# A two-branch state-space kernel: the middle stage of its long convolution in 64x32 and 32x64 pieces without an exchange of halves, transposes in 64x64 quarters, and a new order

## The chip, the cores and the metric

The kernel runs on one core of a Trainium2 chip. The metric is the time of one execution in microseconds of the device (us), of which lower is better. The core has a matrix engine (TensorE: PE for its matmuls, PEld for its weight loads), a vector engine (VectorE, DVE), an activation engine (ScalarE, ACT), a general engine (GpSimd, POOL) and a synchronization engine (SyncE, SP). SP and POOL issue the transfers. The engines run side by side, each through its own instructions in a fixed order, and wait for each other by semaphores.

## The reference, cut to what matters

Two independent branches of 2048 positions by 1024 channels in bfloat16, put side by side in the output:

```python
def _A_ref(q, k, v, shift_k, ssm_k, ssm_D):      # branch A
    # k_shift: k run through a filter of 4 taps along the positions
    kv = k_shift * v
    # convolution of kv with ssm_k along 2048 positions, by a Fourier transform of length 4096
    kv_f = rfft2(pad(kv)); kf_f = rfft2(pad(ssm_k)).transpose(...)
    y = irfft2(kv_f * kf_f)[:S] + kv * ssm_D
    return q * y

def _B_ref(x, Lambda, B, C, log_dt, Dskip):      # branch B
    Bu = einsum("bld,pd->blp", x, B_bar)          # B_bar complex
    h[t] = Lam_bar * h[t - 1] + Bu[t]             # 1024 complex states, 2048 steps
    y = 2.0 * einsum("blp,dp->bld", h, C).real + x * Dskip
```

## The kernel before, in words

**Branch B** works in 16 chunks `i` of 128 positions. A transfer that transposes brings a chunk of x (`x.i`). `U.i.jp.jl` (line 464) multiplies it by B, 16 matmuls of 128x128 by 128 columns, and two of them fill one PSUM bank; `ue` (line 473) copies the bank to SBUF. `r1`, `r2` (lines 487 and 498) turn the states, `sc` (line 504) scans along time, `r3`, `r4` turn them back. The output product by C is `y.i.dh.part` (line 520, whole 128x128 weights) in chunks 0, 1, 2, 14 and 15, and `yq.i.k` (line 538, in quarters of 64x64, four of which run at the same time) in chunks 3 to 13. `ye` (line 556) copies the result, `yst`, `ysp`, `ysh`, `ysg` store it.

The weights of B and C arrive row by row (`bl`, `cl`), are transposed on PE by `bT`, `cT` (both through `tr_`, line 415, eight 128x128 blocks into one bank), and are copied out of PSUM by `bc` (line 431, ACT), `bcv` (DVE) and `cc` (line 439, ACT). Eight of the sixteen blocks of C are transposed by a transfer instead (`cx`, line 437).

**Branch A** does its Fourier transform of 4096 as 128 times 32, in three stages through DRAM.
- First stage. `kvm`, `kva`, `kvb`, `kvc` (lines 588 to 603, DVE) filter k and multiply by v for sixteen groups of positions `n2`; `am` (line 608) transforms them, 4 matmuls a group, `ae` (line 614) copies, `ast` (line 617) stores to `Ys_kv`. The filter `ssm_k` is transposed on PE by `hT` (line 632, eight 128x128 blocks a bank), copied by `hc` (line 637, ACT), transformed by `hm` (line 657, quarters of 64x64), copied by `he` (line 665), stored to `Ys_h` by `hst` (line 668).
- Middle stage, the one that is changed: 16 steps `i` of two groups `g`. `lh`, `lk` load both transforms, `lw` (line 672) loads that step's weights. `s2` (line 688, called as `sh` and `sk`) does the transform of 32 for one group: 4 matmuls of 64x64 by 512 columns, which end in two banks, real and imaginary parts on neighbouring partitions. `she` (line 697) and `ske` (line 704) copy the banks. The complex product needs the filter's parts in both orders, so `sw`, `swp` (line 708; the first issued by POOL, the second by SP) write a second copy with neighbouring partitions exchanged, by a transfer from SBUF to SBUF, two a step. `pr` (line 714, DVE) multiplies both copies by the data's transform, 4096 elements a partition. `sa` (line 726) transforms back, 8 matmuls of 64x64 by 512 columns for a group, two rounds of four. `sae` (line 734) copies, `vst` (line 737) stores to `Vs`.
- Last stage. `vl` loads, `a3` (line 754) transforms, `a3e` (line 761) copies, `qm` (line 763) multiplies by q, `ost`, `osp` store.

**What sets the order.** A table of words, ORDER, is run through in turn, and each word issues its instructions; so it sets the order on every engine, on the transfer queues of SP and POOL too, and it names which of the 8 PSUM banks (`p`), 53 units of SBUF (`a`), 3 state buffers (`h`) and 3 weight buffers (`w`) a task takes. A copy out of PSUM is on ACT, or on DVE where its word ends in `v` (`shev`, `skev`, `saev`, `a3ev`, `uev`, `yev`).

The banks are eight tiles:

```python
banks = [psum.tile([P, 512], F32, name="bank%d" % b, tag="bank%d" % b, bufs=1) for b in range(8)]
```

## Time and profile before

| what | us |
|---|---|
| runs shown | 343.4 and 346.73, median 345.06 |
| profiled execution, from its first to its last instruction | 343.2 |
| PE busy in it | 329.5 (96%) |
| DVE busy | 325.1 (95%) |
| ACT busy | 273.5 (80%) |
| POOL busy | 68.9 (20%) |
| time of the packets on the two transfer queues, as a share of 16 engines' span | 67.5% and 26.8% |

Of the profiled execution no time but its span is given; it lies 0.2 under the faster of the two runs and 1.9 under their median. A row of a group of instructions has its line, its engine, what it writes and reads, the shape, how many there are (x), the busy time of all of them and the mean duration in ns of one. "64*64 64x512" is a matmul of 64 rows by 64 columns of weights whose output is 64 partitions by 512 columns. A view by windows cuts the span into stretches and gives each engine's busy time and its number of instructions there. The timeline merges instructions of one kind that follow each other: start, duration until the last one's end, engine, line, count. A matmul's end is modelled and reaches past the start of the next one; the distance from start to start is what a matmul costs.

### The profile page before, as it was taken

The page shows a single profiled execution, that of the slowest core. Times are in us where ns is not written, and L with a number is a line of the kernel's source. Part 1 is how long each engine was busy: PE and PEld are TensorE (multiplying, and loading weights), DVE is VectorE, ACT ScalarE, POOL GpSimd, SP SyncE. Part 2 cuts the span into 40 slices and gives each one's busy share as a digit, 9 for nine tenths or more (in the row PEclk, how much of TensorE's full clock was granted, in tenths as well). Part 3 has the DMA queues.
Part 4 walks back from the last instruction along what each step waited for, and adds up shares of the span by engine and source line. Part 5 has one row for each costly group of instructions (what it writes and reads, how often), then busy time and mean ns, then how long its engine had stood idle before and what let it go on. Part 6 is the DMA issues. An engine that isn't in the chain of part 4 may idle for free.

```text
span 343.2 us, 11813 instructions
## 1 busy us (share of the span) xinstructions
PE 329.5 (96%) x5086; PEld 230.2 (67%) x5105; DVE 325.1 (95%) x263; ACT 273.5 (80%) x519; POOL 68.9 (20%) x111
## 2 busy tenths in 40 slices
PE   5799999999999999999999999999999999999993
PEld 2799989545955687578956466666585777754441
DVE  4989999999999999999999999999989999999991
ACT  6999999999999886597888968999599885134541
POOL 6000010151614234122202110202020233000031
PEclk9999999999999999999999999999999999999998
DMA  6999999499996889998998999989998999998997
GB/s 177 352 351 208 315 281 283 155 318 365 368 269 198 264 263 295 233 261 343 313 353 282 270 339 212 369 272 311 280 314 276 216 326 378 327 335 284 375 346 274
DMA packets 62592, 100.83 MB, mean 294 GB/s; under 512 B 29422, under 2 KB 31614, under 8 KB 62540
## 3 DMA queue, kind: packets, MB, share of 16 engines
q1 hardware_dynamic: 52764, 66.47, 67.5%
q0 software_dynamic: 9776, 33.60, 26.8%
q8 instruction: 40, 0.66, 0.8%
q14 instruction: 12, 0.10, 0.1%
HBM read 51.82 MB, written 33.55 MB: 249 GB/s over the span
## 4 chain that ended last, share of the span: by engine, by line
PE 74%; ACT 15%; DMA 4%; issue 3%; DVE 3%; SPq 0%; POOL 0%; DVEq 0%; POOLq 0%
PE bank L464 25%; PE bank L538 19%; PE bank L520 10%; PE bank L754 4%; PE bank L688 4%; PE bank L726 4%; PE bank L608 2%; PE bank L657 2%; ACT BT L431 2%; ACT arena L614 2%; ACT arena L473 2%; ACT CT L439 2%; ACT arena L637 2%; DMA wslot<-a_c_W 1%; DMA arena<-arena 1%
## 5 line engine op out<-in xcount | busy, mean ns | idle before, releaser
L464 PEld LDWEIGHTS <-BT 128*128 128x128 bf16 x2048 | 117.8, 98 | 14.4 <-issue 9.9
L464 PE MATMUL bank<-arena,BT 128*128 128x128 bf16 x2048 | 125.4, 221 | 1.1 <-ACT BT L431 0.9
L538 PE MATMUL bank<-CT,gslot 64*64 64x512 bf16 x1408 | 86.6, 378 | 0.0
L504 DVE TENSOR_TENSOR_SCAN gslot<-rtab,gslot 128x1040 bf16<-128x1040 f32 x32 | 73.0, 2311 | 0.5
L538 PEld LDWEIGHTS <-gslot 64*64 64x64 bf16 x1408 | 36.9, 107 | 30.8 <-issue 1.9
L473 ACT CAST arena<-bank 128x512 bf16<-128x512 f32 x63 | 40.5, 660 | 13.8 <-PE bank L464 13.4
L614 ACT CAST arena<-bank 128x512 bf16<-128x512 f32 x64 | 37.2, 680 | 6.7 <-PE bank L608 4.0
L697 ACT CAST arena<-bank 128x512 bf16<-128x512 f32 x63 | 35.0, 617 | 5.9 <-issue 2.8
L520 PE MATMUL bank<-CT,gslot 128*128 128x512 bf16 x153 | 38.5, 380 | 0.3
L665 ACT CAST arena<-bank 128x512 bf16<-128x512 f32 x64 | 35.2, 631 | 3.1 <-PE bank L657 3.0
L714 DVE TENSOR_TENSOR arena<-arena 128x4096 bf16<-128x4096 bf16 x16 | 36.5, 2280 | 1.1 <-DMA arena<-arena 1.0
L487 DVE TENSOR_TENSOR arena<-gslot,Z 128x4096 bf16<-128x4096 bf16 x16 | 36.6, 2287 | 0.8 <-DVE gslot L504 0.2
L704 ACT CAST arena<-bank 128x512 bf16<-128x512 f32 x60 | 34.4, 621 | 3.2 <-PE bank L688 3.0
L734 ACT CAST arena<-bank 128x512 bf16<-128x512 f32 x60 | 32.4, 616 | 5.5 <-PE bank L726 5.3
L487 DVE TENSOR_TENSOR arena<-arena,Z 128x4096 bf16<-128x4096 bf16 x16 | 36.5, 2280 | 0.1
L556 ACT CAST arena<-bank 128x512 bf16<-128x512 f32 x31 | 18.1, 599 | 16.6 <-PE bank L538 8.7
L588 DVE TENSOR_TENSOR arena<-arena 128x4096 bf16<-128x4096 bf16 (+3 forms) x16 | 30.0, 1881 | 0.0
L668 POOL DMA_DIRECT2D Ys_h<-arena x32 | 23.2, 735 | 25.5 <-ACT arena L665 20.2
L617 POOL DMA_DIRECT2D Ys_kv<-arena x16 | 11.2, 726 | 83.5 <-ACT arena L614 81.1
L520 PEld LDWEIGHTS <-gslot 128*128 128x128 bf16 x160 | 14.1, 98 | 15.9 <-issue 2.3
L688 PE MATMUL bank<-arena,wslot 64*64 64x512 bf16 x256 | 21.5, 382 | 0.3 <-DMA wslot<-a_c_W 0.3
L737 POOL DMA_DIRECT2D Vs<-arena x16 | 11.7, 731 | 46.3 <-ACT arena L734 41.3
(105 smaller groups left out, 416.2 us busy)
## 6 DMA issues: line engine op xcount, KB each, us to landing
Ys_kv<-arena POOLq DMA_DIRECT2D x16, 512.0 KB, 5.6
Ys_h<-arena POOLq DMA_DIRECT2D x32, 256.0 KB, 4.6
arena<-Ys_h SPq DMA_DIRECT2D x16, 512.0 KB, 5.0
arena<-Ys_kv SPq DMA_DIRECT2D x16, 512.0 KB, 5.6
Vs<-arena POOLq DMA_DIRECT2D x16, 512.0 KB, 5.6
arena<-Vs SPq DMA_DIRECT2D x16, 512.0 KB, 6.7
arena<-arena SPq DMA_DIRECT2D x17, 256.0 KB, 4.2
arena<-in_A_k_dram SPq DMA_DIRECT2D x8, 512.0 KB, 5.2
```

The costliest lines, as they stand in the source:

```text
L464: nc.tensor.matmul(pu[:, w, jl, :], BT[:, 2 * jp + jl, w, d, :], xT[:, d, :], start=(d == 0), stop=(d == ND - 1))
L473: cp(st["u", i][:, :, 2 * jp:2 * jp + 2, :], st.pop(("pu", i, jp)))
L487: nc.vector.tensor_mul(m, s_, win(Z))
L504: nc.vector.tensor_tensor_scan(gf, rtab[:].rearrange("p j t -> p (j t)"), gf, 0.0, ALU.mult, ALU.add)
L520: nc.tensor.matmul(py, h[:, w, j, 2:GW], CT[:, j, w, dh * 512:(dh + 1) * 512], start=(j == 0 and w == 0), stop=False)
L538: mm = nc.tensor.matmul(st["py", i, dh][cols, cs(r)], lhs(dh, rows, c), rhs(dh, rows), start=first, stop=last)
L614: cp(st["ysb", n2][:, p, dh * 512:(dh + 1) * 512], st.pop(("pa", n2, p, dh)))
L665: cp(o, st.pop(("pb", hf, s, e, r)).rearrange("p (n c t) -> p n c t", n=2, c=2))
L688: nc.tensor.matmul(st["ps", nm, g, l][64 * dh:64 * dh + 64, :], st["w", i][rows, a * WC:a * WC + 64], st[nm, i][rows, a, dh * 512:(dh + 1) ...
L697: cp(st["hab", i][:, 0, a, l, :], st.pop(("ps", "h", g, l)))
L704: cp(st["x16", i][:, a, l, :], st.pop(("ps", "k", g, l)))
L714: nc.vector.tensor_mul(hab, st.pop(("x16", i)).rearrange("p a l d -> p (a l d)").unsqueeze(1).to_broadcast([P, 2, 2 * D]), hab)
```

## The change

**Middle stage.** A step's two groups share their 128 partitions anew: 32 partitions each for the two groups and the two halves of the channels, real and imaginary parts in separate copies (`w`, `z`) along the free dimension. `s2` makes 8 matmuls of 64 rows by 32 columns of weights in place of 4 of 64x64. `she` and `ske` copy as before. `sw` and `swp` are gone, with their 32 transfers. `pr` multiplies the same number of elements and reads both operands with a repeated stretch. `sa` is called once a step in place of once a group, takes four banks at once, and makes 32 matmuls of 32 rows by 64 columns in four rounds of eight. Weights of a step are 512 in place of 640 columns.

**Transposes.** `turn` makes four transposes of 64x64 in place of one of 128x128; the upper and the lower 64 rows go to two neighbouring banks. Two tasks share such a pair of banks, and the copies read both banks at once (`both`, `halves`). `cc` and `hc` get forms on DVE.

**Banks and order.** The eight banks are one tile. ORDER is a new table throughout: of copies out of PSUM on DVE it has 30 in place of 22.

The diff, with both tables, the constants' table of weights and lines that only pass names on left out:

```diff
-WC = 320
+WC = 512
...
-    banks = [psum.tile([P, 512], F32, name="bank%d" % b, tag="bank%d" % b, bufs=1) for b in range(8)]
+    banks = psum.tile([P, 8 * 512], F32, name="banks")
...
     def bank():
-        return banks[cur["p"].pop(0)][:]
+        b = cur["p"].pop(0)
+        return banks[:, b * 512:(b + 1) * 512]
+
+    def bank_pair():
+        b = cur["p"].pop(0)
+        return banks[:].bitcast(BF16)[:, b * 1024:(b + 2) * 1024].rearrange("p (r o) -> p r o", r=2)
+
+    def both(pair, o, n):
+        return pair[:, :, o:o + n * 64].rearrange("p r (n t) -> p n r t", t=64)
+
+    def turn(pair, o, src):
+        for c in range(2):
+            for r in range(2):
+                rows, cols = slice(64 * r, 64 * r + 64), slice(64 * c, 64 * c + 64)
+                nc.tensor.transpose(pair[cols, r, o:o + 64], src[rows, cols], ident[rows, rows])
...
-    def tr_(key, dst_key):
+    def tr_(key, nm, n, w):
         src = st.pop(key)
-        pt = bank16()
+        if (nm, n) not in st:
+            st[nm, n] = bank_pair()
         for d in range(ND):
-            nc.tensor.transpose(pt[:, d, :], src[:, d * P:(d + 1) * P], ident[:])
-        st[dst_key] = pt
+            turn(st[nm, n], 64 * (ND * w + d), src[:, d * P:(d + 1) * P])
+
+    def turned(nm, n, w):
+        return both(st[nm, n], 64 * ND * w, ND)
+
+    def halves(ap):
+        return ap.rearrange("p d (r t) -> p d r t", r=2)
...
-    E["bc"] = lambda j, w: nc.scalar.mul(BT[:, j, w, :, :], st.pop(("bp", j, w)), -1.0 if w else 1.0)
+    E["bc"] = lambda j, w: nc.scalar.mul(halves(BT[:, j, w, :, :]), turned("bp", j, w), -1.0 if w else 1.0)
...
     def hT(hf, s):
-        pt = bank().bitcast(BF16).rearrange("p (n c t) -> p n c t", n=4, c=2)
-        st["ph", hf, s] = pt
+        if ("ph", hf, s // 2) not in st:
+            st["ph", hf, s // 2] = bank_pair()
...
-                nc.tensor.transpose(pt[:, n, c, :], hv[:, 16 * (n // 2) + 2 * s + n % 2, :], ident[:])
+                turn(st["ph", hf, s // 2], 64 * (8 * (s % 2) + 2 * n + c), hv[:, 16 * (n // 2) + 2 * s + n % 2, :])
...
     def s2(nm, g):
-        i, a = divmod(g, 2)
+        i, w = divmod(g, 2)
         for l in range(2):
             st["ps", nm, g, l] = bank()
-        for dh in range(2):
-            for l in range(2):
-                rows = slice(64 * l, 64 * l + 64)
-                nc.tensor.matmul(st["ps", nm, g, l][64 * dh:64 * dh + 64, :], st["w", i][rows, a * WC:a * WC + 64],
-                                 st[nm, i][rows, a, dh * 512:(dh + 1) * 512], start=True, stop=True)
+        for a in range(2):
+            for dh in range(2):
+                for l in range(2):
+                    rows, o = slice(64 * l, 64 * l + 64), 64 * a + 32 * dh
+                    c0 = 64 * a + 32 * w
+                    nc.tensor.matmul(st["ps", nm, g, l][o:o + 32, :], st["w", i][rows, c0:c0 + 32],
+                                     st[nm, i][rows, a, dh * 512:(dh + 1) * 512], start=True, stop=True,
+                                     tile_position=(64 * l, o))
...
-    def swap(dma, i, q):
-        dma(st["hab", i][q:P:2, 1, :, :, :], st["hab", i][1 - q:P:2, 0, :, :, :])
-    E["sw"] = lambda i, q: swap(gpd, i, q)
-    E["swp"] = lambda i, q: swap(spd, i, q)
...
     def pr(i):
-        hab = st["hab", i].rearrange("p t a l d -> p t (a l d)")
-        nc.vector.tensor_mul(hab, st.pop(("x16", i)).rearrange("p a l d -> p (a l d)").unsqueeze(1).to_broadcast([P, 2, 2 * D]), hab)
+        hab = st["hab", i].rearrange("p z w l d -> p z w (l d)")
+        x16 = st.pop(("x16", i)).rearrange("p w l d -> p w (l d)")
+        nc.vector.tensor_mul(hab, x16.unsqueeze(1).to_broadcast([P, 2, 2, D]),
+                             hab[:, :, 1:2, :].to_broadcast([P, 2, 2, D]))
...
-    def sa(g):
-        i, a = divmod(g, 2)
-        for dh in range(2):
-            st["pv", g, dh] = bank()
-        for t in range(2):
+    def sa(i):
+        for g in (2 * i, 2 * i + 1):
+            for dh in range(2):
+                st["pv", g, dh] = bank()
+        passes = ((0, 0, 0), (1, 1, 1), (0, 1, 2), (1, 0, 2))
+        for n, (z, w, t) in enumerate(passes):
             for l in range(2):
-                for dh in range(2):
-                    rows = slice(64 * dh, 64 * dh + 64)
-                    c0 = a * WC + 64 + 128 * l + 64 * t
-                    nc.tensor.matmul(st["pv", g, dh][64 * l:64 * l + 64, :], st["w", i][rows, c0:c0 + 64],
-                                     st["hab", i][rows, t, a, l, :], start=(t == 0), stop=(t == 1))
+                for a in range(2):
+                    for dh in range(2):
+                        r0 = 64 * a + 32 * dh
+                        c0 = 128 + 192 * l + 64 * t
+                        nc.tensor.matmul(st["pv", 2 * i + a, dh][64 * l:64 * l + 64, :], st["w", i][r0:r0 + 32, c0:c0 + 64],
+                                         st["hab", i][r0:r0 + 32, z, w, l, :], start=(n == 0), stop=(n == 3),
+                                         tile_position=(r0, 64 * l))
```

**Where the new table moves instructions.** The first place is ACT's beginning, up to its first copies of branch B's products (line 473 before, 491 after). BT is the transposed B; the rows of lines 360 to 362 (371 to 373) make tables of the turning. Before:

```order
L431 ACTIVATE BT<-bank_99 128x1024
L473 CAST arena<-bank_102 128x2x256
L431 ACTIVATE BT<-bank_96 128x1024
L431 ACTIVATE BT<-bank_98 128x1024
L473 CAST arena<-bank_97 128x2x256
```

After, behind two copies of branch A's first stage (line 632) and fourteen of B (line 448) that stand further up:

```order
L632 CAST arena<-banks 128x512 x3
L456 COPY CT<-banks 128x8x128
L448 ACTIVATE BT<-banks 128x1024 x2
L632 CAST arena<-banks 128x512
L371 CAST Z_78<-arena 128x1024
L372 CAST Z_78<-arena 128x1024
L373 ACTIVATE Z_78<-arena 128x1024
L491 CAST arena<-banks 128x2x256 x2
```

Before, the first copies of products stand among the copies of B; now they stand behind all of these and behind six of branch A (line 632).

The second place is DVE's beginning, behind the small tables (line 342 before, 353 after). Lines 588 to 603 (606 to 621) are the filter of branch A, Z is a table of branch B. Before:

```order
L427 TENSOR_SCALAR BT<-bank_102 128x1024
L588 TENSOR_TENSOR arena<-arena 128x4096
L429 COPY BT<-bank_96 128x1024
L595 TENSOR_TENSOR arena<-arena 128x2048
L601 TENSOR_TENSOR arena<-arena 128x1024
L354 SCALAR_TENSOR_TENSOR Z_77<-arena,b_224 128x128
L355 SCALAR_TENSOR_TENSOR Z_77<-arena,b_224 128x128
```

After:

```order
L457 COPY CT<-banks 128x8x128
L606 TENSOR_TENSOR arena<-arena 128x4096 x3
L613 TENSOR_TENSOR arena<-arena 128x2048 x2
L619 TENSOR_TENSOR arena<-arena 128x1024 x2
L621 TENSOR_TENSOR arena<-arena 128x1024 x2
```

Before, one step of the filter stands ahead of branch B's table; now four groups of positions go through most of it first. PE's order has the first three `am` (line 626), which take what line 621 writes, ahead of its first `U` (line 482) now; before it has seventeen `U` ahead of its first `am`.

The third place is further on in ACT's order. Lines 614 and 632 are `ae`, 665 and 683 `he`, 637 and 655 `hc`, 574 is `ye`; line 518 prepares the next scan. Before:

```order
L637 COPY arena<-bank_98 128x1024
L637 COPY arena<-bank_96 128x1024
L614 CAST arena<-bank_97 128x512
L665 CAST arena<-bank_98 128x4x128
L614 CAST arena<-bank_99 128x512
L665 CAST arena<-bank_101 128x4x128
L614 CAST arena<-bank_98 128x512
```

After:

```order
L518 COPY gslot_90<-gslot_89 128x16
L683 CAST arena<-banks 128x4x128
L655 COPY arena<-banks 128x1024 x2
L683 CAST arena<-banks 128x4x128 x2
L632 CAST arena<-banks 128x512
L574 CAST arena<-banks 128x512
L683 CAST arena<-banks 128x4x128 x3
```

Ahead of the copy to which `L614 CAST arena<-bank_99` belongs, PE's order holds 640 matmuls of `U` and 83 of line 520 (538); ahead of that of the second copy in the row of two of line 683, it holds 512 and 63.

289 lines of the change are left out of this document (144 added, 145 removed).

## The prediction

> **What bounds the kernel now.** I read the page's first part, then the kinds of engine in the chain of waits, then windows.
>
> ```profile
> PE 329.5 (96%) x5086; PEld 230.2 (67%) x5105; DVE 325.1 (95%) x263; ACT 273.5 (80%) x519; POOL 68.9 (20%) x111
> PE 74%; ACT 15%; DMA 4%; issue 3%; DVE 3%; SPq 0%; POOL 0%; DVEq 0%; POOLq 0%
> ```
>
> Two engines are nearly full over the whole span, and the chain runs through PE for 74% of it, though 15% lies on ACT, which is only 80% busy. An average over 343.2 hides stages, so here are the busy times by stretch (start and end, length, then PE, PEld, DVE, ACT, POOL with their instructions, PE's granted clock, transfers' share, GB/s):
>
> ```profile
> 0.00:20.00 20.00, 14.28 (x107) 11.17 (x108) 13.62 (x36) 16.92 (x35) 5.62 (x17) 1.00 0.89 281
> 20.00:40.00 20.00, 19.95 (x355) 19.76 (x354) 19.89 (x29) 19.20 (x26) 0.00 (x0) 1.00 1.17 262
> 40.00:60.00 20.00, 19.50 (x305) 17.79 (x305) 20.00 (x15) 20.00 (x35) 2.11 (x3) 1.00 1.11 299
> 60.00:80.00 20.00, 19.58 (x152) 9.43 (x153) 19.55 (x18) 18.71 (x35) 7.94 (x11) 1.00 0.85 256
> 80.00:100.00 20.00, 19.84 (x246) 15.06 (x248) 19.88 (x16) 19.11 (x37) 6.96 (x10) 1.00 0.94 340
> 0.00:100.00 100.00, 93.15 (x1151) 73.21 (x1161) 92.93 (x111) 93.94 (x162) 22.63 (x41) 1.00 0.99 288
> 100.00:330.00 230.00, 228.33 (x3897) 153.34 (x3904) 226.28 (x148) 176.30 (x353) 43.32 (x66) 1.00 0.94 296
> 330.00:343.20 13.20, 8.00 (x42) 3.70 (x41) 5.92 (x7) 3.30 (x7) 2.95 (x5) 0.90 0.82 299
> ```
>
> From 20 to 100 us three engines are full at once, ACT by 77.0 of 80. Past 100, ACT has 53.7 of idle time, PE 1.7. So there are two regimes: up to about 100 us nothing can go faster than ACT's copies, and from there the end is PE's remaining work plus a tail. A saving on PE counts only when it lies in the second regime. That decides this case: most of what the change saves on PE lies in the first, and the question is how much PE work is left when ACT has done its first 94 us.
>
> **The change part by part.**
>
> *Transposes.* Now:
>
> ```profile
> L415 PE MATMUL bank<-ident,arena 128*128 128x128 bf16 x192 | 16.5, 249 | 1.4 <-ACT BT L431 1.2 <-ACT arena L614 0.2
> L632 PE MATMUL bank<-ident,arena 128*128 128x128 bf16 x128 | 9.8, 227 | 0.1
> ```
>
> 26.3 us of PE. In quarters, four of which run at the same time as `yq` does, they are 1280 that cost something like a third. But every one of them is followed by a copy, and they all lie before the place where ACT's queue lets PE go; the copies keep their number and size (some go to DVE). I count 0; what is saved there is time in which PE waits for ACT.
>
> *The exchange and the weights.* 32 transfers of 256 KB go, 8.4 MB of 100.8, and the weights shrink by a fifth. What waited for them:
>
> ```profile
> DVE arena L714 <- DMA arena<-arena: 1.0, 2, 0.6
> L688 PE MATMUL bank<-arena,wslot 64*64 64x512 bf16 x256 | 21.5, 382 | 0.3 <-DMA wslot<-a_c_W 0.3
> ```
>
> 1.0 and 0.3, hidden behind `U` and `y`, which PE does meanwhile. PE's idle time past 100 us is 1.7 in all, so that is the most this can return. I count 0, since PE has other work at each of these places.
>
> *`pr`.* 16 instructions of 4096 elements as before:
>
> ```profile
> L714 DVE TENSOR_TENSOR arena<-arena 128x4096 bf16<-128x4096 bf16 x16 | 36.5, 2280 | 1.1 <-DMA arena<-arena 1.0
> L761 DVE CAST arena<-bank 128x512 bf16<-128x512 f32 x9 | 5.9, 679 | 0.0
> ```
>
> Both operands now read a repeated stretch. The multiplications of line 487 read repeated stretches too and take 2.28 like this one, so 0. Eight more copies on DVE, 5.9 of busy time for nine in a row of the second form, are +4.8 at 0.60 each from start to start, as an estimate: DVE 329.9. That is work beside PE's, and would bound only a span near 338.
>
> *Middle stage on PE.* `s2` and `sa` keep their work of 64 and 64 passes of 512 columns if eight pieces run side by side as four quarters do: eight matmuls of 64x32 in one pass, eight of 32x64. Bounds: 0 for equal passes; if eight go as two rounds of four, 128 more passes. A pass is read here:
>
> ```profile
> 153.99 1.95 PE L464 MATMUL bank<-arena,BT 128*128 128x128 bf16 x32
> 155.87 0.41 PE L688 MATMUL bank<-arena,wslot 64*64 64x512 bf16 x4
> 156.22 2.85 PE L464 MATMUL bank<-arena,BT 128*128 128x128 bf16 x48
> 159.00 0.63 PE L688 MATMUL bank<-arena,wslot 64*64 64x512 bf16 x8
> 173.06 0.39 PE L538 MATMUL bank<-CT,gslot 64*64 64x512 bf16 x4
> 173.27 0.39 PE L688 MATMUL bank<-arena,wslot 64*64 64x512 bf16 x4
> 173.49 0.82 PE L538 MATMUL bank<-CT,gslot 64*64 64x512 bf16 x12
> ```
>
> Four quarters last 0.215 from start to start (173.06 to 173.27, 173.27 to 173.49), so 128 would be +27.5. I take 0, because four run abreast without loss and the array is filled no further by eight.
>
> *Changes of shape on PE.* These rows give a price that no busy time shows. From line 688 at 155.87 to line 464 at 156.22 are 0.35, of which the pass is 0.215: 0.13. The other way, 48 matmuls of line 464 take 2.78 until line 688 starts (156.22 to 159.00) and 32 take 1.88 (153.99 to 155.87), so one is 0.056 and the change 0.08 to 0.09. From 173.06 to 173.49 line 538 and line 688, both in quarters, follow each other at no cost. I take 0.11 for each change between whole 128x128 and tiled pieces. By PE's order there are 79 such places before, 23 ahead of the place below and 56 behind; in the change 141, 38 ahead and 103 behind. Of these 103, 47 are between 64x64, 64x32 and 32x64, which the trace doesn't have. Bounds for one: 0, as from `yq` to `s2`, and 0.13; I take 0.11, because the rows nearest in kind are those where the shape of a piece changes. 47 x 0.11 = 5.2.
>
> The Trainium skill ("TensorEngine Tiling (Array Packing)", Key Properties) says that a change of tiling mode, and not of the tile alone, drains the array; the 0.11 and the 0 above agree with it, and by it the 47 cost like the others. If the rule held only for whole against tiled, the sum would be 5.2 less.
>
> *The new order.* Here lies the main term. The rows of ACT:
>
> ```profile
> 27.89 3.68 ACT BT L431 x4
> L665 ACT CAST arena<-bank 128x512 bf16<-128x512 f32 x64 | 35.2, 631 | 3.1 <-PE bank L657 3.0
> 5.01 2.05 ACT L408 CAST arena<-bank 128x512 bf16<-128x512 f32 x4
> ```
>
> A copy of 1024 columns takes 0.91 from start to start (3.68 for four), one of 512 takes 0.48 (four end after 2.05, of which the last one's own 0.6 is the tail). With such prices ACT's order before contains 93.5 us of work up to the copy `L614 CAST arena<-bank_99`, which is what it has done at 100 us. In the change, 93.4 us of ACT work end with the second copy in the row of two of line 683. Both orders have done all transposes and the same passes of `hm`, but for one, there, and DVE has 95.2 us of work ahead of either place. What differs is PE's order ahead of it: 640 matmuls of `U` and 83 of `y` before, 512 and 63 in the change. So the same ACT time brings less of branch B's PE work with it: ACT's early time goes to copies of B, of `hT` and of `am`, and `U` comes late. The trace confirms the count for before:
>
> ```profile
> 0.00:100.00 100.00, 41.01 (x640) 38.36 (x640) 1.00 0.99 288
> 100.00:343.20 243.20, 84.35 (x1408) 79.46 (x1408) 0.99 0.93 296
> 0.00:100.00 100.00, 19.25 (x76) 6.91 (x80) 1.00 0.99 288
> ```
>
> (`U` in two stretches, then line 520; weight loads say 80.) Prices of the work that slides behind the place:
>
> ```profile
> 117.68 3.68 PE bank L464 x64
> 65.40 1.03 PE L520 MATMUL bank<-CT,gslot 128*128 128x512 bf16 x4
> 66.26 0.22 PE L523 MATMUL bank<-Dd,arena 128*128 128x128 bf16 x1
> 66.32 1.03 PE L520 MATMUL bank<-CT,gslot 128*128 128x512 bf16 x4
> ```
>
> - 128 of `U` at 0.056 (3.68 for 64 in the chain gives 0.0575 with the last one's end): 7.2
> - 20 of `y` with 5 of the product by D, 0.92 for four and one (65.40 to 66.32): 4.6
> - 103 - 56 = 47 more changes of shape at 0.11: 5.2
>
> Sum 17.0, all of it in a regime where PE has 1.7 of idle time to hide it in.
>
> *What starts it.* Before, the first `U` starts at 14.93, when the first copies of B are there. In the change it stands behind three `am`, which wait for DVE's filter:
>
> ```profile
> 14.93 1.89 PE L464 MATMUL bank<-arena,BT 128*128 128x128 bf16 x16 [0.85 <-ACT BT L431]
> 14.81 2.28 DVE L588 TENSOR_TENSOR arena<-arena 128x4096 bf16<-128x4096 bf16 x1
> 17.61 1.21 DVE L595 TENSOR_TENSOR arena<-arena 128x2048 bf16<-128x2048 bf16 x1
> 20.11 0.69 DVE L601 TENSOR_TENSOR arena<-arena 128x1024 bf16<-128x1024 bf16 x1 [1.28 <-PE bank L415]
> ```
>
> Three, two and three of these in DVE's order are 11.3 at most, and begin at about 14.8: until about 25. Queued behind the first `am` on PE are transposes of B and C, which feed ACT; ACT has its tables and the copies of B already transposed until then (the last four copies of B start at 27.89 before), so I take this wait as covered. If that cover is gone, ACT's end of the first regime moves by the same amount, up to some 4 us; I count 0. The first `U` I expect at about 30 us.
>
> **Sum.** 343.2 + 17.0 = 360.2 on the profiled execution's scale. The two runs shown have a median 1.9 over that span and the faster 0.2 over; I add 0.7: **361**.
>
> **The rivals.**
>
> *B, not slower: PE closes up its gaps.* One mechanism: with the exchange and its waits gone, and the tiled shapes changing free of charge, PE and ACT both run without idle time. Then the 47 changes cost nothing (5.2), ACT's 3.0 of idle time between 20 and 100 us vanish, and PE's 1.7 past 100: 360.2 - 9.9 = 350.3. The point from which it decides is 2% over the median, 352.0. For it: the waits in the lists above are the only ones that PE has in the middle stage, and 0 between `yq` and `s2`. Against: ACT's idle time stems from `U` and `am`, not from the exchange, and the new order has more such switches of supplier.
>
> *C, slower still: eight pieces don't run abreast.* With two rounds of four the middle stage costs +27.5: 388; with half the loss, 374. For it: the trace has no eight. Against: four cost no more than one. The Trainium skill ("TensorE: Matmul & The Clock Gate", Measured speedup vs the span model) gives 10.6 times for sixteen pieces of 32x32; scaled to these shapes as an estimate it would give at most +14, so 374.
>
> *D, faster: PE's savings count and DVE is the bound.* If the 26.3 of the transposes fall to about 9, the order costs nothing, and DVE's idle time shrinks from 18.1 (343.2 - 325.1) to the 8 that its first and last microseconds take anyway, the end is 329.9 + 8 = 338. Against it stands ACT's full stretch; ACT would have to be faster too, and no row says so.
>
> *E: `pr` loses its rate.* If two repeated operands run at half the rate, 16 x 2.28 = +36.5: 397. Against: line 487.
>
> **How the numbers follow.** Forecast 0.63, from about 353 (the tiled changes free and PE's gaps closed, 353.3) to 367 (a start 4 us late, changes at 0.13). B 0.18, C 0.12, D 0.04, E 0.03. The range reaches into B and the half of C: 347 to 375 leaves out D, E and the worse half of C. A measurement of this kernel can tell about 2% from no change. Slower by over 2%: the forecast, C and E, 0.78; within: B, 0.18; faster: D, 0.04.
>
> **What would show it.** Right: in the windows of the changed kernel, PE has done some 512 of `U` at 100 us, not 640; ACT is full up to there; PE is full from there to the end; first `U` near 30 us; eight pieces of `s2` within about 0.22 and changes of shape near 0.1 from start to start; `pr` at 2.28. Wrong: ACT's first 94 us of work ending well before or after 100, PE with idle time past 100 us, a pass of eight that takes over 0.3, or PE's full stretch beginning earlier than 100 us because the cheaper transposes let the banks come free sooner.

## The result, and the profile after

The changed kernel takes 377.33 us in the median of two runs (376.33 and 378.33) against 345.06: a ratio of 1.093 with a 95% interval of 1.079 to 1.108. It is slower, as forecast, but by 32 us where 16 were forecast, and 2.3 us above the end of the range. The profiled execution spans 374.6 us, 31.4 more than before. From here on a median is over all executions of a kernel, while a ratio leaves out those in a slower state of the chip.

The page of the changed kernel, its first part and the kinds of engine in the chain:

```profile
PE 346.1 (92%) x6577; PEld 235.2 (63%) x6577; DVE 332.4 (89%) x271; ACT 271.3 (72%) x511; POOL 60.7 (16%) x97
PE 74%; ACT 10%; DMA 9%; issue 3%; SPq 1%; DVE 1%; POOL 0%; ACTq 0%; POOLq 0%; DVEq 0%
```

PE's busy time has grown by 16.6, and its idle time from 13.7 to 28.5: each is about half of the loss. The windows say where (columns as in the prediction):

```profile
0.00:20.00 20.00, 10.22 (x350) 6.58 (x351) 14.46 (x36) 17.05 (x26) 5.32 (x13) 1.00 0.84 291
20.00:40.00 20.00, 11.43 (x384) 9.04 (x383) 20.00 (x32) 19.81 (x34) 1.01 (x5) 1.00 1.18 232
40.00:60.00 20.00, 18.11 (x384) 15.80 (x384) 15.66 (x12) 15.77 (x27) 2.10 (x3) 0.91 1.02 288
60.00:80.00 20.00, 18.61 (x307) 14.41 (x307) 15.13 (x11) 15.08 (x28) 5.08 (x7) 0.91 0.77 201
80.00:100.00 20.00, 19.41 (x265) 13.54 (x264) 17.48 (x16) 17.40 (x36) 7.60 (x11) 1.00 0.88 278
100.00:200.00 100.00, 99.28 (x1731) 72.36 (x1729) 95.48 (x67) 80.02 (x154) 21.96 (x32) 1.00 0.79 245
200.00:300.00 100.00, 98.82 (x2200) 58.81 (x2192) 92.89 (x61) 75.14 (x151) 10.74 (x16) 1.00 0.68 214
```

From 100 us on PE is full, as forecast. But ACT, which the prediction had full up to its first 93.4 us of work, is full only to 40; from 40 to 100 it stands for 11.8 of 60. The copy at which the prediction cuts the kernel is the last row of each fence, in the timeline of ACT before (first fence) and in the changed kernel (second, the later of two copies):

```profile
101.75 0.69 ACT L614 CAST arena<-bank 128x512 bf16<-128x512 f32 x1
```

```profile
112.03 1.93 ACT L655 COPY arena<-banks 128x1024 bf16<-128x1024 bf16 x2 [0.72 <-PE banks L270]
113.85 1.09 ACT L683 CAST arena<-banks 128x512 bf16<-128x512 f32 x2
```

It ends at 102.4 before and at 114.9 in the changed kernel. Behind it lie 240.8 us before (343.2 - 102.4) and 259.7 now. So the 31.4 are 12.5 ahead of the cut, where the prediction had none, and 18.9 behind it, where it had 17.0. The work behind the cut is what the order had promised; here `U` ahead of 114.3 us and behind, then line 538 ahead of it:

```profile
0.00:114.30 114.30, 34.09 (x512) 31.34 (x512) 0.97 0.91 247
114.30:374.60 260.30, 91.18 (x1536) 86.82 (x1536) 1.00 0.76 245
0.00:114.30 114.30, 15.49 (x64) 5.60 (x64) 0.97 0.91 247
```

512 and 64, against 512 and 63 forecast. What makes PE late ahead of the cut is in its timeline. Here are the two longest stops from 33 to 64 us, each inside a run of `U` (the rows of other lines between them left out), and PE's clock around them:

```profile
34.33 3.69 PE L482 MATMUL banks<-arena,BT 128*128 128x128 bf16 x63
40.41 3.03 PE L482 MATMUL banks<-arena,BT 128*128 128x128 bf16 x33 [2.38 <-issue]
...
59.14 0.45 PE L482 MATMUL banks<-arena,BT 128*128 128x128 bf16 x5
61.39 2.85 PE L482 MATMUL banks<-arena,BT 128*128 128x128 bf16 x27 [1.80 <-issue]
```

```profile
36.00:40.00 4.00, 2.02 (x37) 1.85 (x34) 4.00 (x7) 4.00 (x5) 0.00 (x0) 1.00 1.27 144
40.00:44.00 4.00, 3.60 (x35) 3.13 (x36) 1.93 (x3) 2.69 (x5) 0.00 (x0) 0.65 1.04 300
58.00:62.00 4.00, 2.20 (x60) 1.89 (x58) 3.39 (x2) 2.98 (x4) 0.00 (x0) 0.96 1.05 408
62.00:66.00 4.00, 4.00 (x78) 3.61 (x79) 3.93 (x6) 1.68 (x4) 0.00 (x0) 0.62 1.24 188
```

A `U` is 16 matmuls, and nothing that it waits for comes after its first ones; yet PE stops behind the 63rd and the fifth, and the view names no releaser but "issue". After each stop the granted clock is low. The trace holds the loads of PE's own instructions too: each brings 16 KB, and one ran from 37.23 to 39.02 us, another from 59.08 to 60.09, so that by the same records PE went on 1.3 to 1.4 us after the end of each. That they are PE's is read from their number: its matmuls and weight loads, 6577 of each, are 51.4 times 256 instructions. The page counts the loads, before and in the changed kernel:

```profile
q8 instruction: 40, 0.66, 0.8%
```

```profile
q8 instruction: 51, 0.84, 0.9%
```

The list of PE's waits up to the cut has five such stops in the changed kernel, 6.5 us together, and each ends 1.3 to 1.4 us after the end of a load; before it has none:

```profile
PE banks L482 <- issue: 4.2, 2, 2.4
PE banks L270 <- issue: 2.3, 3, 1.2
```

The pieces of the middle stage themselves run as counted. 16 matmuls of 64x32 are two passes of eight, 32 of 32x64 are four:

```profile
169.37 0.39 PE L556 MATMUL banks<-CT,gslot 64*64 64x512 bf16 x4
169.69 0.63 PE L708 MATMUL banks<-arena,wslot 64*32 64x512 bf16 x16
170.24 1.96 PE L482 MATMUL banks<-arena,BT 128*128 128x128 bf16 x32
...
209.44 1.07 PE L746 MATMUL banks<-arena,wslot 32*64 32x512 bf16 x32
210.44 0.41 PE L708 MATMUL banks<-arena,wslot 64*32 64x512 bf16 x8
```

From 169.69 to 170.24 are 0.55 for two passes of 0.215 and a change of 0.12. From 169.37 to 169.69 are 0.32 for one pass of quarters and the change to 64x32: 0.10, where quarters to quarters cost nothing. The 1.00 from 209.44 to 210.44 are four passes and 0.14 for the change from 32x64 to 64x32.

The groups by form show the product at its old rate and the transposes at no lower busy time than the 26.3 of before:

```profile
L731 DVE TENSOR_TENSOR arena<-arena 128x4096 bf16<-128x4096 bf16 x16 | 36.4, 2286 | 2.8 <-ACT arena L725 2.2 <-ACT arena L718 0.4
L270 PE MATMUL banks<-ident,arena 64*64 64x64 bf16 x1280 | 28.5, 246 | 8.5 <-ACT CT L456 3.1 <-issue 2.3 <-DMA arena<-in_B_B_re_dram 1.3
```

### The profile page after: what moved, and what is told of

Same layout as the page of the kernel before. It is cut to its first block, busy times and chain, and to the rows that moved or that the text cites. A ratio compares the mean times of both kernels' runs of the same rounds, so it can differ in the third digit from the quotient of the medians.

```text
span 374.6 us, 14695 instructions
## 1 busy us (share of the span) xinstructions
PE 346.1 (92%) x6577; PEld 235.2 (63%) x6577; DVE 332.4 (89%) x271; ACT 271.3 (72%) x511; POOL 60.7 (16%) x97
## 4 chain that ended last, share of the span: by engine, by line
PE 74%; ACT 10%; DMA 9%; issue 3%; SPq 1%; DVE 1%; POOL 0%; ACTq 0%; POOLq 0%; DVEq 0%
PE banks L482 24%; PE banks L556 20%; PE banks L538 8%; PE banks L270 4%; DMA arena<-in_A_ssm_k_dram 4%; PE banks L708 4%; PE banks L746 4%; PE banks L775 4%; ACT BT L448 3%; PE banks L626 3%; DMA arena<-Vs 2%; PE banks L675 2%; DMA Ys_h<-arena 1%; DMA Vs<-arena 1%; ACT arena L419 1%
## 5 line engine op out<-in xcount | busy, mean ns | idle before, releaser
L482 PE MATMUL banks<-arena,BT 128*128 128x128 bf16 x2048 | 125.3, 221 | 4.5 <-issue 4.2
L556 PE MATMUL banks<-CT,gslot 64*64 64x512 bf16 x1408 | 84.7, 378 | 0.9 <-ACT arena L725 0.8
L556 PEld LDWEIGHTS <-gslot 64*64 64x64 bf16 x1408 | 34.8, 107 | 34.4 <-issue 8.2
L491 ACT CAST arena<-banks 128x512 bf16<-128x512 f32 x62 | 37.1, 612 | 25.9 <-PE banks L482 25.8
L755 ACT CAST arena<-banks 128x512 bf16<-128x512 f32 x60 | 31.9, 613 | 11.0 <-PE banks L746 11.0
L538 PE MATMUL banks<-CT,gslot 128*128 128x512 bf16 x160 | 38.5, 379 | 0.0
L683 ACT CAST arena<-banks 128x512 bf16<-128x512 f32 x64 | 34.1, 627 | 4.1 <-PE banks L675 2.3
L632 ACT CAST arena<-banks 128x512 bf16<-128x512 f32 x64 | 34.6, 629 | 3.2 <-issue 1.6
L270 PE MATMUL banks<-ident,arena 64*64 64x64 bf16 x1280 | 28.5, 246 | 8.5 <-ACT CT L456 3.1
L718 ACT CAST arena<-banks 128x512 bf16<-128x512 f32 x58 | 31.2, 603 | 5.6 <-PE banks L708 5.5
L574 ACT CAST arena<-banks 128x512 bf16<-128x512 f32 x28 | 16.6, 602 | 25.5 <-PE banks L556 13.6
L270 PEld LDWEIGHTS <-arena 64*64 64x64 bf16 x1280 | 26.7, 165 | 12.7 <-issue 8.6
L725 ACT CAST arena<-banks 128x512 bf16<-128x512 f32 x57 | 30.6, 617 | 5.4 <-PE banks L708 5.4
L626 PE MATMUL banks<-arena,F1t 128*128 128x512 bf16 x64 | 19.2, 404 | 6.3 <-ACT BT L448 5.0
```

The lines of the kernel that those rows point to most:

```text
L270: nc.tensor.transpose(pair[cols, r, o:o + 64], src[rows, cols], ident[rows, rows])
L482: nc.tensor.matmul(pu[:, w, jl, :], BT[:, 2 * jp + jl, w, d, :], xT[:, d, :], start=(d == 0), stop=(d == ND - 1))
L491: cp(st["u", i][:, :, 2 * jp:2 * jp + 2, :], st.pop(("pu", i, jp)))
L538: nc.tensor.matmul(py, h[:, w, j, 2:GW], CT[:, j, w, dh * 512:(dh + 1) * 512], start=(j == 0 and w == 0), stop=False)
L556: mm = nc.tensor.matmul(st["py", i, dh][cols, cs(r)], lhs(dh, rows, c), rhs(dh, rows), start=first, stop=last)
L632: cp(st["ysb", n2][:, p, dh * 512:(dh + 1) * 512], st.pop(("pa", n2, p, dh)))
```

## The experiments

Two theories of the 12.5 ahead of the cut: **supply** (the quarters use up four times as many instructions as whole blocks, and PE stands for the next 16 KB of them) and **start** (the order puts branch A's filter ahead of the first `U`, which starts at 31.68 us in place of 14.93, so PE is late for good). And three parts to price apart: transposes, pieces, order. Times are medians, ratios are to the kernel before in the same runs.

### Whole transposes in the changed kernel (e1_whole)

```diff
     def turn(pair, o, src):
-        for c in range(2):
-            for r in range(2):
-                rows, cols = slice(64 * r, 64 * r + 64), slice(64 * c, 64 * c + 64)
-                nc.tensor.transpose(pair[cols, r, o:o + 64], src[rows, cols], ident[rows, rows])
+        n = o % 512 // 64
+        nc.tensor.transpose(pair[:, o // 512, P * n:P * n + P], src, ident[:])
```

(and the view that the copies read)

> The changed kernel with transposes of whole 128x128 blocks again (320 in place of 1280; same order, banks, copies and middle stage). Supply theory: PE stands still because its instructions arrive in blocks of 16 KB and the quarters use up four times as many instructions for the same work; with whole blocks the stops of 0.6 to 4.6 us beside those loads, and the half-speed clock after two of them, go, and the kernel falls to 358 to 366. Start theory: PE is late because its order puts the filter of branch A ahead of the first U; the transposes do not matter, 372 to 380, and the copy at which the prediction cuts the kernel stays near 114 us. The prediction's own sum (17 behind that copy, which is reached at 100) would give about 361 with whole blocks.

Measured: 367.5 us, ratio 1.071 [1.065, 1.076]; the profiled execution spans 361.4. ACT's copy at the cut, PE's wait for the filter and the first `U` in it:

```profile
100.13 1.09 ACT L681 CAST arena<-banks 128x512 bf16<-128x512 f32 x2
```

```profile
26.82 1.01 PE L624 MATMUL banks<-arena,F1t 128*128 128x512 bf16 x2 [5.73 <-ACT BT L446]
...
31.87 1.06 PE L480 MATMUL banks<-arena,BT 128*128 128x128 bf16 x16
```

The median is a little over the 358 to 366 of the supply theory, 10 under the changed kernel; the traced execution, at 363.2, is the fastest of four. The cut says it clearly: it ends at 101.2, about where the prediction had it, although PE waits 5.73 for the filter and the first `U` comes as late as in the changed kernel. The start theory falls: that late start is covered. That the quarters are the cause of the 12.5 is shown by this; that it is all the supply of instructions is not, as the runs with quarters in one place alone tell. Behind the cut are 260.2, as in the changed kernel.

### Half transposes (e2_half)

```diff
-        for c in range(2):
-            for r in range(2):
-                rows, cols = slice(64 * r, 64 * r + 64), slice(64 * c, 64 * c + 64)
-                nc.tensor.transpose(pair[cols, r, o:o + 64], src[rows, cols], ident[rows, rows])
+        for r in range(2):
+            rows = slice(64 * r, 64 * r + 64)
+            nc.tensor.transpose(pair[:, r, o:o + 64], src[rows, :], ident[rows, rows])
```

> The changed kernel with transposes of 64 rows by 128 columns, two for a block (640 in place of 1280). Supply theory: in between whole and quarter blocks, 362 to 371. Start theory: as the changed kernel, 372 to 380. If the bank pair and not the number of instructions mattered, it would be as the changed kernel too, while whole blocks, which take one bank each, would be faster.

Measured: 366.6 us, ratio 1.064 [1.058, 1.071], as with whole blocks, not between. It takes the same pair of banks as the quarters, so that pair is not the cause. And twice the instructions cost nothing where four times cost 10 us: not a price for each instruction, but one that begins at a point. PE's list of waits has no stop on issue here.

### Four strips for a transpose in the kernel before (e3_strips)

```diff
-            nc.tensor.transpose(pt[:, d, :], src[:, d * P:(d + 1) * P], ident[:])
+            for c in range(0, P, 32):
+                nc.tensor.transpose(pt[c:c + 32, d, :], src[:, d * P + c:d * P + c + 32], ident[:], tile_position=(0, c))
```

(the same for the filter's)

> The kernel before with each transpose in four strips of 128 rows by 32 columns into the same bank (1280 in place of 320; order, banks and middle stage as before). Supply theory: 1920 more PE instructions in the first 100 us, so stops of PE beside the loads of its instructions appear there: 350 to 362. Start theory: 44 more changes of shape at about 0.1 in a stretch in which ACT is full, 345 to 349.

Measured: 357.7 us, ratio 1.039 [1.034, 1.045]. In the kernel before, with its order, its middle stage and one bank for a transpose, cutting the transposes in four alone costs 13 us. PE's list of waits has 4.7 us of stops on issue up to the cut; what the 44 added changes of shape and the lower clock have of the rest is not taken apart. The same kind of stop appears inside `U`, and the copies about the cut come 11 to 12 us late (of line 615, which is line 614 of before):

```profile
35.34 2.24 PE L465 MATMUL bank<-arena,BT 128*128 128x128 bf16 x37
40.35 1.83 PE L465 MATMUL bank<-arena,BT 128*128 128x128 bf16 x30 [2.77 <-issue]
```

```profile
112.83 0.59 ACT L615 CAST arena<-bank 128x512 bf16<-128x512 f32 x1 [0.39 <-PE bank L609]
```

### Quarters for the filter alone, and for B and C alone (e6_q_filter, e7_q_bc)

The changed kernel with `turn1`, the whole transpose of e1_whole, at one of its two callers:

```diff
-            turn(st[nm, n], 64 * (ND * w + d), src[:, d * P:(d + 1) * P])
+            turn1(st[nm, n], 64 * (ND * w + d), src[:, d * P:(d + 1) * P])
```

> The changed kernel with the transposes of B and C in whole blocks (192) and those of the filter ssm_k in quarters (512). Supply theory: stops of PE of 1 to 2 us beside loads of instructions only where the filter is transposed, from 50 us on; part of the 10 us between e1_whole and the changed kernel: 369 to 374. If the loss comes from the first 30 us alone, 366 to 369.

> The changed kernel with the filter's transposes in whole blocks (128) and those of B and C in quarters (768). Supply theory: stops beside loads of instructions from 10 to 40 us, and the rest of the 10 us: 370 to 375. If early stops are covered by ACT, which has its queue full until 40 us, 366 to 369, and then the loss is the filter's.

Measured: 371.7 us (ratio 1.083 [1.079, 1.087]) with the filter's in quarters, 369.1 (1.074 [1.070, 1.078]) with those of B and C. In the trace of e6_q_filter the copy at the cut ends at 110.7, in that of e7_q_bc at 105.4: 9.5 and 4.2 later than with whole blocks, 13.7 together; with both it is 114.9, 13.7 later. By the medians the two parts are 4 and 2 us over e1_whole, 6 of the 10, so that they seem to add up at the cut is partly chance: the traced execution of e6_q_filter is the slowest of its four. Both say that the 512 of the filter cost more than the 768 of B and C, which begin while ACT has its queue full.

The stops fit the supply theory in e7_q_bc, 6.5 us on issue up to the cut. In e6_q_filter they don't: the stops of 1 to 2 us beside loads that were expected are not there, and PE's list has 0.6 on issue. What ACT waits for there, up to the cut, and e1_whole's list does not have:

```profile
ACT arena L499 <- DMA Ys_kv<-arena: 4.3, 1, 4.3
ACT arena L663 <- PE banks L278: 2.6, 4, 1.3
```

The first is one wait that ends with a store of branch A's first stage; the changed kernel has none for it. The second are the filter's quarters (line 278 in that run), and these are slow themselves. Here are 32 of the filter's blocks in quarters in the changed kernel, then 16 in halves in e2_half and 16 whole in e1_whole, all at a clock of 1.00:

```profile
103.98 3.81 PE L270 MATMUL banks<-ident,arena 64*64 64x64 bf16 x128
```

```profile
50.44 1.23 PE L269 MATMUL banks<-ident,arena 64*128 64x64 bf16 x32
```

```profile
50.45 1.25 PE L268 MATMUL banks<-ident,arena 128*128 128x128 bf16 x16
```

For 16 blocks that is 1.9 us in quarters and 1.2 in halves or whole. The filter's blocks are read from positions 32 apart, those of B and C from neighbouring ones; whether that is the reason is not shown. The changed kernel has both costs in ACT's list up to the cut, waits for `U` with its stops and for the filter's quarters:

```profile
ACT arena L491 <- PE banks L482: 7.2, 5, 3.3
ACT arena L655 <- PE banks L270: 4.2, 5, 1.4
```

### A burst of transposes behind the end (e8_burst)

```diff
+        for n in range(512):
+            for c in range(2):
+                for r in range(2):
+                    rows, cols, o = slice(64 * r, 64 * r + 64), slice(64 * c, 64 * c + 64), 64 * (n % 16)
+                    nc.tensor.transpose(pt[r][cols, o:o + 64], ident[rows, cols], ident[rows, rows])
```

> The kernel before with 2048 transposes of 64x64 of a constant put behind its end, with nothing to wait for and hardly any transfers under way; their results are not used. It measures the pace at which PE gets instructions. If nothing limits it but the array, about 0.012 each as in the runs of 65 in the changed kernel: 25 us in all. Supply theory: runs of some 128 (256 instructions, one block of 16 KB) with stops between them, 0.016 to 0.024 each: 33 to 50 us in all.

Measured: a span of 395.3 us. The timeline of PE in the burst:

```profile
342.84 1.92 PE L793 MATMUL bank<-ident 64*64 64x64 bf16 x128 [3.23 <-issue]
346.30 1.92 PE L793 MATMUL bank<-ident 64*64 64x64 bf16 x128 [1.53 <-issue]
...
390.22 1.92 PE L793 MATMUL bank<-ident 64*64 64x64 bf16 x128 [1.81 <-issue]
```

Runs of exactly 128 matmuls, each with its weight load: 256 instructions, 16 KB at 64 bytes. Then a stop of 1.5 to 2.1. From 342.84 to 390.22 are 13 runs, 3.64 each, with almost no transfers under way (5 GB/s or less). So in the burst PE gets 256 instructions in 3.6 us and no more. The runs of 128 are as expected; the pace is 0.028 for a transpose where 0.016 to 0.024 was expected, and over 51 us in all against 33 to 50.

In the changed kernel a block needed longer still. The 65 quarters from 33.66 and the 63 of `U` behind them are 128 pairs, one block, which lasted until 38.02, 4.36 us, and yet PE stopped for 2.38 more. The next load started 3.6 us after the block's beginning, where in the burst most start 1.1 after it. What delayed it is not shown; other transfers were under way (a share of 1.27 from 36 to 40 us, against 0.02 in the burst).

What a block of instructions lasts, if it is all transposes of B and C that run undisturbed, is read from PE's timeline at the same place: in the changed kernel, in e2_half and in e1_whole.

```profile
33.66 0.74 PE L270 MATMUL banks<-ident,arena 64*64 64x64 bf16 x65 [0.55 <-issue]
```

```profile
32.88 0.90 PE L269 MATMUL banks<-ident,arena 64*128 64x64 bf16 x48
```

```profile
32.76 1.50 PE L268 MATMUL banks<-ident,arena 128*128 128x128 bf16 x24
```

So 128 quarters last 1.5 us (128 x 0.74 / 65), 128 halves 2.4 and 128 whole ones 8.0; 128 of `U` last 7.2. Whole blocks and `U` last longer than the burst's 3.6, quarters and halves of B and C don't; 128 quarters of the filter, at 3.8, do. That halves still cost nothing is then in part that the filter's are no slower than whole blocks, and for B and C a matter of how many come in a row: 32 blocks are 64 halves, half a load's worth, and PE waits for copies or data before the next; as quarters they are 128, a whole one. This last step is argued from the counts, not shown.

The Trainium skill ("Runtime: NRT & Kernel Launch", Instruction fetch mechanics) has the instructions refilled in 16 KiB blocks of 256, which these runs of 128 pairs show. It adds that the cost of crossing such a boundary is mostly hidden. That holds in the kernel before; in the burst it is 1.5 to 2.1 us at every boundary.

### Pieces of 64x64 with the new order (e5_square)

e1_whole with the middle stage's matmuls in 64x64, which leaves out the exchange of parts:

```diff
-        for a in range(2):
-            for dh in range(2):
-                for l in range(2):
-                    rows, o = slice(64 * l, 64 * l + 64), 64 * a + 32 * dh
-                    ...
+        for dh in range(2):
+            for l in range(2):
+                rows = slice(64 * l, 64 * l + 64)
+                nc.tensor.matmul(st["ps", nm, g, l][64 * dh:64 * dh + 64, :], st["w", i][rows, 64 * w:64 * w + 64],
+                                 st[nm, i][rows, w, dh * 512:(dh + 1) * 512], start=True, stop=True)
```

(`sa` likewise)

> The changed kernel with whole transposes (as in e1_whole) and with the middle stage's matmuls in pieces of 64x64: as many passes of 512 columns, half as many matmuls, 81 changes of shape in place of 128; copies, pr and all transfers as in the changed kernel. It leaves out the exchange of parts, so the numbers that it computes in branch A are others. It shows the new order without the new pieces. If the new order costs what the prediction said (128 of U and 20 of y more behind the place at 100 us: 11 to 12) and the pieces the rest, 356 to 362 by the median. If the new order costs nothing by itself and the pieces are all of it, 344 to 349. If the pieces cost nothing, 366 to 369 as e1_whole.

Measured: 363.1 us, ratio 1.048 [1.044, 1.051]. So the new order, with whole transposes, no exchange and no new pieces, costs 4.8%, some 16 us. 11 to 12 were expected: by the median it is just outside the 356 to 362, by the ratio (1.048 times 343.6 is 360) inside. What leaving out the exchange does in it is not told apart. The pieces on top are the rest to e1_whole, 2.3% by the ratios (8 us) and 4 us by the medians; 47 changes at 0.10 are 4.7 of it.

### The new pieces with the old order (e4_middle)

```diff
-sa.1:p4p2 sa.0:p1p3
+sa.0:p1p3p4p2
```

(this for each step, with the functions of the change's middle stage; the words of the exchange go)

> The kernel before with the new middle stage alone (pieces of 64x32 and 32x64, no exchange, one transform back a step; the order of before, in which the second of a step's two words for it does the whole and the copies of the first wait for it). Theory that the pieces cost nothing but changes of shape: 149 in place of 79 at 0.10 each are +7, so 350 to 353. Rival, the exchange had cost something that the profile doesn't show as a wait (its 8.4 MB and its place on two queues): 340 to 346. Rival, the pieces lose their rate: over 357.

Measured: 362.0 us, ratio 1.051 [1.047, 1.055]: more than the 350 to 353 of the changes of shape alone, and in the range of the rival by which the pieces lose their rate. They don't: as in the changed kernel 32 matmuls of 32x64 with one change take 1.00, here from 206.59 to 207.59. The trace gives 4.4 of it to one wait of PE for a step's weights, at 284 us.

### Without the exchange, and the weights asked for earlier (e9, e10, e11, e12)

e9_no_exchange is the kernel before with the words `sw`, `swp` left out and `pr` as in the change; the pieces stay 64x64.

```diff
-    E["sw"] = lambda i, q: swap(gpd, i, q)
-    E["swp"] = lambda i, q: swap(spd, i, q)
...
-        nc.vector.tensor_mul(hab, st.pop(("x16", i)).rearrange("p a l d -> p (a l d)").unsqueeze(1).to_broadcast([P, 2, 2 * D]), hab)
+        nc.vector.tensor_mul(hab, x16.unsqueeze(1).to_broadcast([P, 2, 2, D]),
+                             hab[:, :, 1:2, :].to_broadcast([P, 2, 2, D]))
```

Like e5_square it computes the middle stage without the exchange of parts.

> The kernel before without its 32 exchanges and with the smaller weights; the product reads both operands with a repeated stretch as in the changed kernel, and the middle stage's matmuls keep their 64x64 pieces and their order. It leaves out the exchange, so the numbers of branch A are others. It shows what the exchange itself had cost. Prediction's count: nothing, since the waits for it are 1.0 in all beside a full PE: 342 to 345. Rival, its transfers and its places on two queues cost something that no wait shows: under 340. What e4_middle has over this run is the price of the pieces in the old order.

Measured: 352.9 us, ratio 1.023 [1.018, 1.029]. Taking 8.4 MB of transfers away makes it slower, against both expectations; whether by 2% is unclear from the interval. The main place is one wait:

```profile
PE bank L681 <- DMA wslot<-a_c_W: 6.7, 1, 6.7
```

and SP's queue shows why. First before, then e9_no_exchange:

```profile
267.36 0.54 SPq L708 DMA_DIRECT2D arena<-arena  x1
267.94 0.59 SPq L672 DMA_DIRECT2D wslot<-a_c_W  x1
271.79 0.47 SPq L708 DMA_DIRECT2D arena<-arena  x1
```

```profile
268.46 1.51 SPq L665 DMA_DIRECT2D wslot<-a_c_W  x1
270.08 3.69 SPq L736 DMA_DIRECT2D arena<-in_A_q_dram  x3
```

Before, SP stood at the exchange until 271.79, so the three loads of q, 512 KB each, went out later. Without it they follow the weights at once, and the weights land 12.8 us after their issue, where the median of such loads in this run is 3.4. Three more runs tried to mend it. In e11_no_exchange_w13 and e12_middle_w13 (the latter is e4_middle with this) step 13's weights are asked for ahead of step 14's, some 40 words earlier than they were; in e10_middle_lw step 14's are asked for 16 words earlier in e4_middle. The first two:

```diff
-r1.12:a2 sae.31.0:a28 saev.30.1
-saev.31.1 lw.14:w0 sk.24:p6p2 ske.24.0:a7
+lw.13:w2 r1.12:a2 sae.31.0:a28 saev.30.1
+saev.31.1 lw.14:w0 sk.24:p6p2 ske.24.0:a7
```

> e4_middle with the load of one step's weights (step 14) asked for 16 words earlier in the order, right behind the last reader of its buffer. In e4_middle PE stands for 4.4 us at 283 us until these weights land. If that wait is part of what the pieces cost there, 356 to 359; if another transfer is late in its place, 360 to 363.

Measured: 363.8 us, ratio 1.055 [1.049, 1.062] against 360 to 363 at the most, and the wait is 4.2 in place of 4.4. By PE's order the late weights are those of step 13, not of step 14.

> e9_no_exchange (exchange left out, so branch A's numbers are others) with one word moved: the weights of step 13 are asked for 44 words earlier, ahead of a load of x and of the loads of q instead of behind. In e9_no_exchange PE stands 6.9 us for these weights at 274 us and its clock is at half for 6.8 us after it. Theory: the exchange had been holding back SP's queue, without it the loads of q go out at once and this small transfer lands late among them; asked for earlier, it costs nothing: 342 to 346, so that the exchange itself had cost nothing. Rival: another transfer is late in its place, 350 to 354.

Measured: 347.5 us, ratio 1.011 [1.008, 1.015], 1.5 over the expected 342 to 346; the wait is 2.5 in place of 6.7, and now for step 14's weights. So by the ratios 4 of the 8 us were this one load's place in SP's queue.

> e4_middle with the same word moved. If the 4.4 us wait at 283 us goes, 356 to 359; what stays over e11_no_exchange_w13 is then the price of the pieces of 64x32 and 32x64 in the old order: 70 changes of shape at 0.10 (7) and about 2 for passes of eight. If it stays at 361 to 364, the wait has moved.

Measured: 362.2 us, ratio 1.050 [1.042, 1.058], and the wait is still 4.4: it moved to step 14's weights. Over e11_no_exchange_w13 the pieces cost 3.9% in the old order, about 14 us. 7 are changes of shape, 2 more the difference of the two waits; the rest is not taken apart here.

## Why the prediction was wrong

**What bounds the kernel** was right for the kernel before, and with whole transposes: two regimes, ACT's queue up to the cut, then PE. In the changed kernel ACT is not full up to the cut, and its first 94 us of work end 15 later than at 100, which the prediction had named as a sign of being wrong.

**Transposes: the step that failed.** The prediction said that 1280 quarters "cost something like a third", and counted 0 because "what is saved there is time in which PE waits for ACT". It asked whether a saving there could count, never whether it could be a loss. Quarters cost 28.5 of busy time, not a third of 26.3, and PE stops beside them. They cost 12.5 us at the cut in the changed kernel (114.9 against 102.4); whole blocks bring it to 101.2. Two things are behind it. One is the supply of instructions, a resource that no row of before showed at its limit: there the loads lie 4.3 us or more apart and PE never stops on issue; in the changed kernel it does for 6.5 us up to the cut, and the clock is low after the longest two. The other is the rate of the filter's quarters, 1.9 us for 16 blocks where whole ones take 1.2, for which ACT waits 4.2. How the 12.5 divide between the two is not shown. No rival had this side either: C and E were losses of rate in the middle stage.

**The order** was right in kind, and in size by the traces. Ahead of the cut stand 512 of `U` and 64 of `y`, as counted, and behind it 18.9 us more than before, against 17.0. e1_whole, which is the change without the step that failed, spans 361.4; the forecast for the change was 360.2 on that scale. But that is its fastest execution. By its median it is 23 us over the kernel before, where the sum had 17.0: by the ratio of e5_square 16 are the order (11.8 in the sum), the rest the pieces (5.2). What the surplus consists of is not shown.

**Changes of shape** were right: 0.10 to 0.14 each in the rows above, also between tiled shapes. The rule of the Trainium skill ("TensorEngine Tiling (Array Packing)", Key Properties) that a change of mode drains the array agrees with these prices; rival B, which had the 47 for nothing, falls.

**Passes of eight** run at the rate of four: 32 matmuls of 32x64 in 1.00 with one change, so rival C falls. `pr` took 2.286, so rival E falls.

**The exchange** counted as 0 agrees with the changed kernel, whose PE waits for no weights; no run has the new order with it. In the old order 0 is not right: taking it out cost 2.3%, half of it because SP's queue was no longer held back.

**The late first U**, 31.68 against about 30 forecast, was covered as the prediction said; e1_whole shows it.

**The scale**: the profiled execution's time is 376.33 for a span of 374.6, 1.7 more and not 0.7, and the median is 1.0 above that. So by the traces the miss of 16.3 (377.3 against 361) is 12.5 ahead of the cut, 1.9 behind it and 2.0 of scale. By the medians whole transposes take back only 9.8 of it.

## What to carry to other kernels

Splitting a matmul into smaller ones that run side by side saves array time but multiplies instructions; price a run of small ones by what brings them, at best 256 in 3.6 us in this case and at one place in the kernel 6.75, and time a small one of each kind: four quarters of the filter took longer than its whole block, four of B or C did not. When an edit is counted as 0 because its saving is hidden, ask separately what its loss would cost. And a transfer that is taken off an in-order queue lets all behind it go earlier: look at which small one then lands late.

## What the runs showed of the hardware

- Instructions of PE come in blocks of 256; in a burst with hardly any other traffic one block took 3.64 us from start to start, of which 1.92 was work at half clock (e8_burst). In the changed kernel a block of 4.36 us of work still ended in a stop of 2.38.
- Transposes of 16 blocks of the filter took 1.25 us whole, 1.23 in halves and 1.9 in quarters.
- A change of shape on PE cost 0.10 to 0.14 us, also from 64x64 to 64x32 and from 32x64 to 64x32; passes of eight pieces took 0.215 like passes of four.
- After a stop of about 2 us the granted clock was 0.65 and 0.62 over the next 4 us (changed kernel); a stop costs more than its own length.
- A transfer of 128 KB landed 12.8 us after its issue when three of 512 KB followed it in the queue (e9_no_exchange).
